# One scan and one step on r put ahead of the low part of a weight tile on VectorE, in a gated linear attention with an ELU feed-forward

## The chip, the cores and the metric

The kernel runs on one core of one Trainium2 chip. The metric is the device time in microseconds (us) of one execution; times of several executions are given as their median. Four engines compute: TensorE (PE in the rows, its weight loads PEld), VectorE (DVE), ScalarE (ACT) and GpSimd (POOL). SyncE (SP) issues nearly all DMAs.

## The reference

```python
B, H, S, D = 4, 8, 768, 48              # q, k, v, alpha: float32 (B, H, S, D)
for t in range(S):
    state = alpha[:, :, t, :, None] * state + einsum('bhd,bhe->bhde', k[:, :, t], v[:, :, t])
    y[:, :, t] = einsum('bhd,bhde->bhe', q[:, :, t], state)
x = y.transpose(0, 2, 1, 3).reshape(B * S, H * D)       # 3072 x 384
h = x @ w_in                                            # w_in 384 x 2048
g = where(h > 0, h, exp(minimum(h, 0)) - 1)
out = g @ w_out                                         # w_out 2048 x 384
```

The weights arrive as float64.

## The kernel before

**Tiling.** The attention is cut into 24 windows of 128 tokens, six for each batch entry. A window's step is named by two letters and its number i: L.i loads k, q and alpha; SC.i (L299, VectorE) makes P, the running products of alpha, by one scan; LN.i and EX.i (L311, L317, ScalarE) make R = 1/P; KA.i, KB.i and KC.i (L325, L330, L335) scale k; PC.i (L340, ScalarE) goes over P once more and keeps the sum of each partition for a check at the end; SQ.i scales q by P; U, S, MK, Y are the small matrix products and the mask, and UA, UB, UC (L509, L538, VectorE) carry the state on. The tokens then go through the feed-forward in nine blocks b, three of 256 tokens and six of 384, and each block over sixteen parts j of the 2048 inner columns (eight pairs in the narrow blocks): A.b.j (L786, TensorE) writes h into a PSUM bank, RA (L795) and RB (L800) on ScalarE make r = exp(min(h, 0)), RC (L806, VectorE) makes max(r - 1, h), GH (L812, ScalarE) and GL (L819, VectorE or GpSimd) split it into a high and a low part, and O.b.j (L835, TensorE) multiplies by w_out.

**Weights.** Sixteen tiles f: F.f loads the raw 64-bit words (L675), KW, DA and DB (L686, L702, L707) turn them into float32 in a tile called wm or spare, WH.f (L734, ScalarE) writes the high part and WL.f (L754, VectorE or GpSimd) the low part. F.13 and F.15 go into the memory of the tile spare and so wait until WL.9 and WL.11 have read it.

**What sets the order.** The order of the steps is a table written out by hand, the string ORDER. Its words are issued one after the other, each to its engine, and no scheduler changes the order on an engine. Two more strings say which of eight PSUM banks and which of eleven SBUF slots each tile takes. Around the change:

- A.1.4 takes the PSUM bank that held h of A.0.6, so TensorE may start A.1.4 when RC.0.6 has read it.
- P has two buffers. The scans stand in the order SC.3, SC.5, SC.4, SC.6, so SC.6 writes into the buffer of window 5. The last to read P of window 5 are SQ.5 on GpSimd and PC.5 on ScalarE.
- WLV (L43) puts WL.11 on VectorE and WL.9, WL.12, WL.14 on GpSimd.

```python
work = main.enter_context(tc.tile_pool(name="work", bufs=2))
...
        d["P"] = work.tile([128, NP, AW], F32, name="P", tag="P")            # SC
...
    nc.scalar.activation(out=win[i]["R"], in_=pw(i), func=AF.Copy, accum_out=chk_p[:, 1, i:i + 1])   # PC
...
    d["g"] = d["r"] if inr(b, j) else d["h"]                                 # RC
    nc.vector.scalar_tensor_tensor(out=d["g"], in0=d["r"], scalar=-1.0, in1=d["h"], op0=ALU.add, op1=ALU.max)
```

Of the kernel before, what the change touches and what calls it, by code (L numbers as in the profile page):

```python
# [15 lines left out]
B, H, S, D = 4, 8, 768, 48  # L16
# [51 lines left out]
CA.1 RC.1.2 KA.4 WH.5 WL.8 O.1.1 GH.1.2 WL.5 RA.1.3 RB.1.3 GL.1.2 A.1.5 RC.1.3 GH.0.3 F.14 ZV.6 KW.6 DA.6 CB.1 F.11  # L68
A.0.4 O.1.2 RA.0.4 RB.0.4 A.0.5 RA.1.5 O.0.2 KB.4 DB.6 WH.14 GL.0.3 SQ.4 KC.4 S.4 WH.12 RB.1.5 RA.0.5 RC.0.4 L.6 KC.5
RC.1.5 DA.5 GH.0.4 KW.5 LV.6 MK.4 TP.4 RB.0.5 GH.1.5 RC.0.5 KN.4 TP.5 KN.5 LC.3 DB.5 GH.1.3 O.0.3 PC.4 SQ.5 CA.3 LV.5  # L70
U.5 WH.9 WL.12 S.5 MK.5.1 MK.5.0 A.0.6 WH.11 WL.11 RA.0.6 GL.1.3 O.1.3 LV.4 U.4 RB.0.6 RC.0.6 PC.5 CB.3 SC.6 WL.9 LN.6
EX.6 GL.0.4 A.1.4 RA.1.4 RB.1.4 UA.4 UB.4 UC.4 L.7 SC.7 LN.7 KA.6 LC.2 RC.1.4 WL.14 A.1.6 KB.6 A.1.7 UA.5 GH.0.5 O.0.4
EX.7 KA.7 KB.7 RA.1.7 KC.6 RA.1.6 RB.1.7 RC.1.7 F.13 GH.1.4 GH.0.6 Y.5 RB.1.6 KC.7 T.7.2 GL.1.5 XH.5 Y.4 PC.7 RC.1.6
XH.4 XL.4 TP.6 GL.1.4 O.1.4 KN.6 F.15 DA.7 KW.7 O.1.5 U.6 UA.6 XL.5 DB.7 PC.6 SQ.6 S.6 MK.6.1 CA.2 GH.1.6 WH.13 GL.0.5
# [1021 lines left out]
```

## Time and profile before

| | |
|---|---|
| median of 3 runs | 463.38 us (463.38 to 463.59) |
| the profiled execution | 463.46 us, its span 461.7 us |
| TensorE busy | 453.9 us, 98% |
| VectorE busy | 349.6 us, 76% |
| ScalarE busy | 327.8 us, 71% |
| GpSimd busy | 214.5 us, 46% |
| granted TensorE clock, mean | 0.999 |

The span runs from the first to the last instruction of the profiled execution; 463.46 us is the time of that same execution with what lies around the span. Shares are over the whole span, so a full engine in one stretch and an empty one in another can give the same share. The times in the rows below count from the start of the span.

### The profile page before, as it was taken

The page shows a single profiled execution, that of the slowest core. Times are in us where ns is not written, and L with a number is a line of the kernel's source. Part 1 is how long each engine was busy: PE and PEld are TensorE (multiplying, and loading weights), DVE is VectorE, ACT ScalarE, POOL GpSimd, SP SyncE. Part 2 cuts the span into 40 slices and gives each one's busy share as a digit, 9 for nine tenths or more (in the row PEclk, how much of TensorE's full clock was granted, in tenths as well). Part 3 has the DMA queues.
Part 4 walks back from the last instruction along what each step waited for, and adds up shares of the span by engine and source line. Part 5 has one row for each costly group of instructions (what it writes and reads, how often), then busy time and mean ns, then how long its engine had stood idle before and what let it go on. Part 6 is the DMA issues. An engine that isn't in the chain of part 4 may idle for free.

```text
span 461.7 us, 12448 instructions
## 1 busy us (share of the span) xinstructions
PE 453.9 (98%) x4942; PEld 439.6 (95%) x4942; DVE 349.6 (76%) x756; ACT 327.8 (71%) x741; POOL 214.5 (46%) x185
## 2 busy tenths in 40 slices
PE   8999999999999999999999999999999999999996
PEld 4889999999999999999999999999999999999995
DVE  8989999999998979978888987898688643211431
ACT  4789997966655767776684976786867568647742
POOL 2224597668647557660744542672434031211140
PEclk9999999999999999999999999999999999999999
DMA  8997744353370535314154425424241311112101
GB/s 280 415 411 287 287 104 156 158 154 103 100 239 0 183 107 173 133 43 140 44 177 142 124 67 181 148 78 155 78 121 35 121 45 53 30 39 85 36 4 57
DMA packets 23859, 61.10 MB, mean 132 GB/s; under 512 B 3184, under 2 KB 10864, under 8 KB 23792
## 3 DMA queue, kind: packets, MB, share of 16 engines
q1 hardware_dynamic: 23360, 59.63, 38.6%
q8 instruction: 41, 0.67, 0.6%
q10 hardware_dynamic: 432, 0.59, 0.3%
q14 instruction: 26, 0.21, 0.2%
HBM read 53.52 MB, written 4.72 MB: 126 GB/s over the span
## 4 chain that ended last, share of the span: by engine, by line
PE 84%; ACT 6%; DVE 5%; issue 1%; DVEq 0%; ACTq 0%
PE o L835 37%; PE h L786 37%; PE y L556 4%; PE q L427 2%; PE q L472 2%; ACT w L734 1%; PE y L551 1%; ACT raw L686 1%; ACT r L800 1%; DVE raw L702 1%; DVE wm L707 1%; ACT gh L812 1%; ACT r L795 1%; DVE r L806 0%; DVE w L754 0%
## 5 line engine op out<-in xcount | busy, mean ns | idle before, releaser
L786 PE MATMUL h<-xt,w 128*128 128x384 f32 (+1 forms) x1296 | 199.9, 310 | 0.3 <-DVE r L806 0.3
L786 PEld LDWEIGHTS h<-xt,w 128*128 128x128 f32 x1296 | 190.7, 190 | 1.5 <-DVE r L806 0.4
L835 PE MATMUL o<-w,gh 128*128 128x384 f32 x768 | 188.3, 327 | 0.0
L819 POOL TENSOR_TENSOR gl<-r,gh 128x384 fp32r<-128x384 f32 (+1 forms) x90 | 106.7, 1193 | 157.7 <-ACT gh L812 101.3
L835 PEld LDWEIGHTS o<-w,gh 128*128 128x128 f32 x768 | 134.1, 189 | 0.5
L835 PE MATMUL o<-w,gl 128*128 128x384 f32 x384 | 125.2, 326 | 0.0
L795 ACT ACTIVATE r<-h 128x384 f32<-128x384 f32 (+1 forms) x120 | 60.4, 510 | 54.9 <-PE h L786 49.0
L388 DVE STREAM_TRANSPOSE kn<-qka 32x128 f32<-32x128 f32 x256 | 77.4, 303 | 4.2
L806 DVE SCALAR_TENSOR_TENSOR r<-r,h 128x384 f32<-128x384 f32 (+1 forms) x90 | 51.1, 578 | 37.7 <-ACT r L800 31.3
L835 PEld LDWEIGHTS o<-w,gl 128*128 128x128 f32 x384 | 72.6, 189 | 0.1
L800 ACT ACTIVATE r<-r 128x384 f32<-128x384 f32 (+1 forms) x120 | 64.1, 543 | 2.0
L812 ACT CAST gh<-r 128x384 fp32r<-128x384 f32 (+1 forms) x90 | 46.4, 529 | 18.5 <-DVE r L806 16.0
L356 POOL TENSOR_TENSOR st<-qka,P 64x512 f32<-64x512 f32 x34 | 43.0, 1265 | 17.4 <-DVE P L299 16.1
L455 DVE TENSOR_TENSOR st<-q,mask 64x256 f32<-64x256 f32 x76 | 32.1, 422 | 9.2 <-PE q L427 6.0
L325 POOL TENSOR_TENSOR qka<-qka,R 128x512 f32<-128x512 f32 x16 | 21.1, 1316 | 29.9 <-ACT R L317 24.7
L806 DVE SCALAR_TENSOR_TENSOR h<-r,h 128x384 f32<-128x384 f32 (+1 forms) x30 | 17.4, 586 | 20.8 <-ACT r L800 20.3
L299 DVE TENSOR_TENSOR_SCAN P<-qka,first 128x516 f32<-128x516 f32 (+1 forms) x25 | 30.7, 1232 | 0.5 <-DMA qka<-in_qka_dram 0.2
L819 DVE TENSOR_TENSOR gl<-h,gh 128x384 fp32r<-128x384 f32 (+1 forms) x30 | 17.3, 581 | 17.8 <-ACT gh L812 7.3
L725 ACT ACTIVATE ck<-ck,lim 128x384 f32<-128x384 int32 x32 | 25.7, 802 | 0.6
L720 ACT ACTIVATE ck<-ck,lim 128x384 int32<-128x384 int8 x32 | 25.4, 794 | 0.0
L311 ACT ACTIVATE R<-P 128x512 f32<-128x512 f32 (+1 forms) x25 | 15.4, 616 | 11.7 <-DVE P L299 11.6
L812 ACT CAST gh<-h 128x384 fp32r<-128x384 f32 (+1 forms) x30 | 14.8, 498 | 8.8 <-DVE h L806 7.9
(95 smaller groups left out, 455.4 us busy)
## 6 DMA issues: line engine op xcount, KB each, us to landing
qka<-in_qka_dram SPq DMA_DIRECT2D x18, 770.0 KB, 6.5
ck<-in_wgt_dram SPq DMA_DIRECT2D x32, 384.0 KB, 3.2
raw<-in_wgt_dram SPq DMA_DIRECT2D x16, 767.6 KB, 9.5
vs<-in_vv_dram SPq DMA_DIRECT2D x42, 192.0 KB, 3.8
out_dram<-ot SPq DMA_DIRECT2D x21, 192.0 KB, 1.9
qka<-in_qka_dram SPq DMA_DIRECT2D x4, 514.0 KB, 4.9
qka<-in_qka_dram SPq DMA_DIRECT2D x8, 256.0 KB, 3.8
xt<-y SPq DMA_DIRECT2D x40, 48.0 KB, 2.5
```

Of the source, the lines that this page charges most:

```text
L299: nc.vector.tensor_tensor_scan(out=P[:, n].rearrange("p n w -> p (n w)"), data0=t[:, 2 * NP * W + n.start * AW:2 * NP * W + n.stop * AW], ...
L356: eng(SQV, i).tensor_tensor(out=st[r, a], in0=d["q"][r], in1=pw(i)[r], op=ALU.mult)
L388: nc.vector.transpose(out=kn[32 * t:32 * t + 32, :, 32 * g:32 * g + 32], in_=d["kt"][32 * g:32 * g + 32, :, 32 * t:32 * t + 32])
L455: nc.vector.tensor_tensor(out=d["st"][r, a, :, c * C:(c + 1) * C], in0=d["s4"][a][o], in1=mask[o].unsqueeze(1).broadcast_to([64, NP, C]), ...
L725: nc.scalar.activation(out=t[:, :, 1].bitcast(F32), in_=t[:, :, 0], func=AF.Square, bias=lim[:, 1:2], accum_out=chk_w[:, f:f + 1])
L786: nc.tensor.matmul(h[:, y, :], lhsT=t[:, wi, ws], rhs=x[:, c, xi].rearrange("p (a x) -> p x a", a=2), start=(y == 0 and k == 0), stop=(k = ...
L795: nc.scalar.activation(out=r, in_=d["h"], func=AF.Relu, scale=-1.0)
L800: nc.scalar.activation(out=d["r"], in_=d["r"], func=AF.Exp, scale=-1.0)
L806: nc.vector.scalar_tensor_tensor(out=d["g"], in0=d["r"], scalar=-1.0, in1=d["h"], op0=ALU.add, op1=ALU.max)
L812: nc.scalar.copy(out=gh, in_=d["g"])
L819: q.tensor_tensor(out=gl, in0=d["g"], in1=d["gh"].bitcast(F32), op=ALU.subtract)
L835: nc.tensor.matmul(o[:, 0:DM], lhsT=gt[:, y, ms], rhs=t[:, wi, f * DM:f * DM + DM].rearrange("p (a x) -> p x a", a=2), start=(u == 0 and y ...
```

## The change

On VectorE, three neighbouring instructions change their order. Before: the low part of weight tile 11 (WL.11), the step on r of block 0, part 6 (RC.0.6), the scan of window 6 (SC.6). After: SC.6, RC.0.6, WL.11. In the table of words SC.6 moves ahead of RB.0.6 and so also ahead of PC.5, which stood before it; on every other engine the order of the instructions stays the same.

```diff
-U.5 WH.9 WL.12 S.5 MK.5.1 MK.5.0 A.0.6 WH.11 WL.11 RA.0.6 GL.1.3 O.1.3 LV.4 U.4 RB.0.6 RC.0.6 PC.5 CB.3 SC.6 WL.9 LN.6
+U.5 WH.9 WL.12 S.5 MK.5.1 MK.5.0 A.0.6 WH.11 RA.0.6 GL.1.3 O.1.3 LV.4 U.4 SC.6 RB.0.6 RC.0.6 WL.11 PC.5 CB.3 WL.9 LN.6
```

VectorE before, from the last mask of window 5 to the step UC.4; names carry their buffer numbers, the brackets name the engines and DMA queues whose semaphores an instruction waits for, and the scan (L299) is listed under its instruction's form:

```order
L455 TENSOR_TENSOR st_1083<-q_1102,mask_87 64x4x64
L754 TENSOR_TENSOR w5_1098<-spare7_476,w5_1098 128x768 [waits DVE_49,Activation_49]
L806 SCALAR_TENSOR_TENSOR r_1144<-r_1144,h_1123 128x512 [waits PE_49,Activation_49]
L299 SCALAR_TENSOR_TENSOR P_1183<-qka0_125,first_91 128x516 [waits DMAHW2_49,Activation_49,Pool_49]
L509 TENSOR_TENSOR vs0_109<-vs0_109,q_1161 128x192 [waits PE_49]
L509 TENSOR_TENSOR q_1162<-vs0_109,q_1162 128x192 [waits DVE_49,PE_49]
L538 TENSOR_TENSOR vs1_110<-q_1162,P_710 48x192 [waits DVE_49]
```

The same place in the change:

```order
L455 TENSOR_TENSOR st_1083<-q_1102,mask_87 64x4x64
L299 SCALAR_TENSOR_TENSOR P_1178<-qka0_125,first_91 128x516 [waits DMAHW2_49,Activation_49,Pool_49]
L806 SCALAR_TENSOR_TENSOR r_1143<-r_1143,h_1123 128x512 [waits PE_49]
L754 TENSOR_TENSOR w5_1098<-spare7_476,w5_1098 128x768 [waits DVE_49]
L509 TENSOR_TENSOR vs0_109<-vs0_109,q_1160 128x192 [waits PE_49]
L509 TENSOR_TENSOR q_1161<-vs0_109,q_1161 128x192 [waits DVE_49,PE_49]
L538 TENSOR_TENSOR vs1_110<-q_1161,P_710 48x192 [waits DVE_49]
```

The scan keeps its three waits and now stands first; the step on r and the low part stand behind it and no longer name ScalarE (Activation) themselves.

ScalarE in the change, from the high parts of tiles 9 and 11 to LN.6 of window 6 (P_605 is P of window 5, P_1178 that of window 6); the order is the same as before:

```order
L734 CAST w5_1098<-spare7_476 128x768
L795 ACTIVATE r_1143<-h_1123 128x512 [waits PE_49]
L800 ACTIVATE r_1143<-r_1143 128x512 [waits Activation_49]
L340 ACTIVATE R_712,chk_p_118<-P_605 128x512 [waits Pool_49]
L725 ACTIVATE ck_1065,chk_w_117<-ck_1065,lim_122 128x384
L311 ACTIVATE R_1186<-P_1178 128x512 [waits DVE_49]
```

PC.5 (L340, reading P_605) stands behind RB.0.6 (L800) and ahead of LN.6 (L311); nothing moved here.

## Rows read from the trace of the kernel before

**Rows 1.** Busy time by engine in four stretches: us, then busy us of each engine, granted clock
```profile
core 0: us, PE busy (x) PEld busy (x) DVE busy (x) ACT busy (x) POOL busy (x), PEclk, DMA share, GB/s
77.03:77.32 0.29, 0.00 (x2) 0.00 (x1) 0.29 (x2) 0.01 (x1) 0.29 (x1) 1.00 0.00 0
77.32:110.00 32.68, 32.68 (x368) 32.03 (x369) 31.48 (x60) 23.44 (x50) 24.16 (x17) 1.00 0.43 150
110.00:200.00 90.00, 90.00 (x1127) 88.08 (x1126) 80.59 (x197) 62.26 (x154) 57.23 (x50) 1.00 0.41 132
200.00:457.30 257.30, 257.30 (x2429) 253.67 (x2427) 167.15 (x403) 176.75 (x418) 95.64 (x87) 1.00 0.28 87
```

**Rows 2.** Chain that ended last, 74 to 84 us: start, us, what
```profile
74.13 0.40 DVE st L455
74.53 0.06 issue
74.59 1.84 DVE w L754
76.43 0.15 issue
76.58 0.70 DVE r L806
77.28 0.04 issue
77.32 6.29 PE h L786 x54
```

**Rows 3.** Timeline of TensorE, 76 to 89 us: start, us, operation, idle before and releaser
```profile
76.35 0.68 PE L472 MATMUL q<-vs,kn 64*64 64x48 f32 x32
77.32 6.29 PE L786 MATMUL h<-xt,w 128*128 128x256 f32 x54 [0.29 <-DVE r L806]
...
85.50 1.15 PE L556 MATMUL y<-st,vs 128*64 128x64 f32 x32
```

**Rows 4.** Timeline of ScalarE around the change
```profile
75.14 0.63 ACT L800 ACTIVATE r<-r 128x512 f32<-128x512 f32 x1
75.67 0.62 ACT L340 ACTIVATE R<-P 128x512 f32<-128x512 f32 x1
76.20 0.18 ACT L340 ACTIVATION_READ_ACCUMULATOR R<-P 128x1 f32 x1
...
78.80 0.64 ACT L311 ACTIVATE R<-P 128x512 f32<-128x512 f32 x1 [1.76 <-DVE P L299]
...
89.94 2.41 ACT L686 ACTIVATE raw<-raw 128x1536 int32<-128x1536 uint8 x1
```

**Rows 5.** Timeline of VectorE, 74 to 83 us
```profile
74.59 1.96 DVE L754 TENSOR_TENSOR w<-spare,w 128x768 fp32r<-128x768 f32 x1
76.58 0.69 DVE L806 SCALAR_TENSOR_TENSOR r<-r,h 128x512 f32<-128x512 f32 x1
77.18 1.59 DVE L299 TENSOR_TENSOR_SCAN P<-qka,first 128x516 f32<-128x516 f32 x1
78.69 0.32 DVE L509 TENSOR_TENSOR vs<-vs,q 128x192 f32<-128x192 f32 x1
...
80.28 1.23 DVE L299 TENSOR_TENSOR_SCAN P<-qka,first 128x516 f32<-128x516 f32 x1
81.42 0.67 DVE L325 TENSOR_TENSOR qka<-qka,R 128x512 f32<-128x512 f32 x1
82.12 0.69 DVE L806 SCALAR_TENSOR_TENSOR r<-r,h 128x512 f32<-128x512 f32 x1
82.73 0.73 DVE L509 TENSOR_TENSOR vs<-vs,q 48x192 f32<-48x192 f32 x2
```

**Rows 6.** Timeline of GpSimd: the three around the change, and one product alone
```profile
73.90 1.83 POOL L754 TENSOR_TENSOR w<-spare,w 128x768 fp32r<-128x768 f32 x1
75.69 1.99 POOL L819 TENSOR_TENSOR gl<-r,gh 128x512 fp32r<-128x512 f32 x1
77.64 2.76 POOL L754 TENSOR_TENSOR w<-wm,w 128x768 fp32r<-128x768 f32 x1
...
96.85 1.29 POOL L819 TENSOR_TENSOR gl<-r,gh 128x512 fp32r<-128x512 f32 x1 [0.34 <-POOL gl L819]
```

**Rows 7.** Timeline of VectorE at 54 us: a low part with GpSimd idle
```profile
54.31 0.95 DVE L754 TENSOR_TENSOR w<-spare,w 128x768 fp32r<-128x768 f32 x1
```

**Rows 8.** Timeline of SyncE: DMA issues behind the low part
```profile
77.50 0.84 SPq L675 DMA_DIRECT2D raw<-in_wgt_dram  x2
```

**Rows 9.** The tile raw, 60 to 120 us: its DMAs from issue to landing
```profile
DMA to landing us min/median/max: 4.4/5.2/5.9
```
## The prediction

> **What bounds the kernel now.** I first read the busy time by stretches. From 77.32 to 457.30 us TensorE is busy in every microsecond of each of the three stretches [rows 1]: 32.68 of 32.68, 90.00 of 90.00, 257.30 of 257.30, at a granted clock of 1.00. There is no slack after 77.32 us into which a late start could vanish. So whatever moves TensorE's start at 77.32 us should move the end by the same amount, in either direction.
>
> Next comes the chain that ended last. Just ahead of 77.32 it does not run over TensorE but over VectorE: the last mask, then the low part of weight tile 11 (WL.11, 1.84), then the step on r (RC.0.6, 0.70), then TensorE's A.1.4 [rows 2]. TensorE had finished its work before at 76.35 + 0.68 = 77.03 and stood idle for 0.29 us for that step [rows 3]. This is the place of the change: the step on r is what releases TensorE, and the change takes the 1.96 us of WL.11 [rows 5] from in front of it and puts a scan there instead.
>
> Then I read what the scan itself must wait for. Before, that could not be seen: SC.6 started at 77.18, at once behind the step on r. Its instruction names ScalarE and GpSimd beside its DMA. P has two buffers, SC.6 writes into the buffer of window 5, and the last reader on ScalarE is PC.5, which stands there behind RB.0.6. The instruction rows of the change agree: with the scan in front, the step on r no longer names ScalarE although it needs RB.0.6, so the scan's own wait must reach at least as far as RB.0.6. PC.5 starts at 75.67 and its accumulator is read out until 76.20 + 0.18 = 76.38 [rows 4]. ScalarE there depends on TensorE and on itself, not on the three moved instructions, so this time stays.
>
> **The change part by part.** It adds and removes no instruction; each of the three moved steps is one VectorE instruction and issues no DMA. The times below are those of the profiled execution (463.46 us, 0.08 above the median of 463.38).
>
> 1. *The scan waits.* VectorE is free for it at 74.59, where WL.11 stood [rows 5]. It can start only behind PC.5: 76.38 + 0.03 = 76.41, the 0.03 being the step from the end of the old scan (77.18 + 1.59 = 78.77) to LN.6 at 78.80 [rows 4, 5]. VectorE stands empty for 1.82 us, with the step on r and WL.11 queued behind the waiting scan.
>
> 2. *The scan's length.* It has two ends: 1.23 as at 80.28, start to start 81.42 - 80.28 = 1.14, and 1.59 as at 77.18, start to start 1.51 [rows 5]. The difference lies on GpSimd. At 77.18 GpSimd's product GL.0.4 ran until 75.69 + 1.99 = 77.68 [rows 6], and the scan ended at 78.77, that is 1.09 later: the 1.23 of a scan alone less 0.14 that it had already spent. WL.11 shows the same: GpSimd's WL.9 ended at 75.73, and WL.11, 0.95 alone [rows 7], ended at 76.55, 0.82 later. And GL.0.4, 1.29 alone [rows 6], ended 1.13 behind WL.11. So of two operations that read two operands from SBUF, the second one waits for the first, less some 0.15 us of its own start. After the change GL.0.4 starts at the same 75.69 (it waits for TensorE), has VectorE idle beside it, and ends at 75.69 + 1.29 = 76.98. The scan then ends at 76.98 + 1.09 = 78.07.
>    The Trainium skill has this rule in SBUF — State Buffer, "SBUF: two separate sides": VectorE's second read interface is GpSimd's too, and whoever starts first keeps it for the whole instruction while the other "fully blocks". The trace differs by the 0.14 above, in three pairs; taken to the letter it is a rival below.
>
> 3. *The step on r and TensorE.* The next instruction starts 0.08 before the end of the scan (78.69 against 78.77), so at 77.99; it takes 0.69 (77.27 in the old place) and TensorE starts 0.05 later [rows 3, 5]: 77.99 + 0.69 + 0.05 = 78.73, against 77.32. **TensorE starts 1.41 us later.** Its 0.29 us of idle time becomes 1.70. RB.0.6, which the step also needs, ended at 75.77 [rows 4] and no longer matters.
>
> 4. *The low part, now last.* It starts 0.09 before the end of the step, at 78.59. GpSimd's WL.14 (1.83, as WL.9 [rows 6]) is ready at 76.94 (0.04 before the end of the product ahead of it, as at 77.64), is held by the scan until 78.07 and ends near 79.7 (the old one ended at 80.40, 1.63 behind the old scan). WL.11 then ends at 79.70 + 0.82 = 80.52, and the state step UA.4 runs from 80.44 to 80.76, against 78.69 to 79.01 [rows 5]. TensorE's A.1.6 takes the bank that UA.4 reads. A.1.4 lasts a third of the 6.29 us for 54 products [rows 3], 2.10, so A.1.6 is due at 78.73 + 2.10 = 80.83 and UA.4 lets it go at 80.76 + 0.05 = 80.81. No wait comes on top, by 0.02 us; I keep 0 to 0.2 for the range.
>
> 5. *What else hangs on these.* VectorE stays 1.75 us late from there, TensorE 1.41, so TensorE's later waits lose 0.34 of their slack. The next is Y.5 at 85.50, which needs the state step that ended at 82.73 + 0.73 = 83.46 [rows 3, 5]: 2.0 us of slack. The DMAs F.13 and F.15 wait for WL.11, and the next load of k, q and alpha is queued behind them on SyncE; they were issued at 77.50 [rows 8] and now near 80.55 to 81.4. They land 4.4 to 5.9 us after issue [rows 9], by 87.3, and ScalarE opens them at 89.94 [rows 4] or later. Cost nothing. LN.6 starts near 78.1 instead of 78.80 [rows 4]; the RA.1.4 behind it waits for TensorE anyway.
>
> Sum: 463.46 + 1.41 = 464.87, and against the median **464.8 us** (463.38 + 1.41 = 464.79). The bounds of the scan's length: start to start 1.14 gives 76.41 + 1.14 + 0.69 + 0.05 = 78.29, +0.97, 464.35; the other end is the first rival. I take the value in step 2 since GpSimd's GL.0.4 is running when the scan becomes ready.
>
> **The rivals.**
>
> *The block is complete.* With no start saved, the scan ends at 76.98 + 1.23 = 78.21, TensorE starts at 78.87 (+1.55); WL.14 ends at 80.04, WL.11 at 80.99, UA.4 at 81.23, and A.1.6, due at 80.97, starts at 81.28: 0.31 more, +1.86 in all, 465.2. Against it: three pairs that each ended 0.13 to 0.16 earlier than that.
>
> *GpSimd goes first.* At 76.98 the scan has been waiting since 76.41, and GpSimd's WL.14 comes. If WL.14 took the turn, it would end at 76.94 + 1.83 = 78.77, the scan at 79.86, and TensorE would start at 79.78 + 0.69 + 0.05 = 80.52, +3.20, 466.6. Against it: at 77.68 the waiting scan went ahead of WL.14, which then took 2.76 [rows 6].
>
> *The scan does not wait* (the change does what the new order suggests). If its ScalarE wait were for something earlier than PC.5, the scan would start at 74.59 and, unhindered, be followed at 75.80 by the step on r (RB.0.6 ends at 75.77), which would end at 76.49, before TensorE needs it at 77.03. The 0.29 us of idle time would go: 463.1, not slower. The point that decides is whether the wait lies before 75.77 or behind it. For it: the rows name only the engine, not the instruction. Against it: the step on r has dropped its ScalarE wait, and the buffer's last reader is PC.5.
>
> *Part of it comes back.* TensorE could run later parts with fewer gaps. Its weight loads are not quite as full as its products, 32.03 of 32.68 in the first stretch [rows 1]. Those gaps recur where it changes from one kind of product to another and none is a wait that an earlier VectorE would end. A return of half, 464.1, is the most I would grant.
>
> **How the numbers follow.** Forecast (scan held by PC.5, +0.97 to +1.6): 0.76, its own range 464.3 to 465.0. Complete block, 465.2: 0.08. GpSimd first, 466.6: 0.04. No wait, 463.1: 0.08. Part back, near 464.1: 0.04. The range 464.1 to 465.5 holds the forecast, the complete block and part of the last case, and leaves out the no-wait case and GpSimd first. A measurement of this kernel can tell about 0.2% from no change, 0.93 us, so slower begins at 464.31. Slower: 0.76 + 0.08 + 0.04, less 0.03 for the lower edge of the forecast, 0.85. Within 0.2%: 0.08 + 0.04 and that 0.03, less 0.02, 0.13. Faster by more than that would take a gain of 0.93 us where TensorE idles 0.29: 0.02.
>
> **What would show it.** In the profile after: VectorE idle from about 74.55 to 76.4, ended by ScalarE's L340; the scan at 76.4 for about 1.65; the step on r at 78.0; TensorE's wait for it about 1.7 instead of 0.29, and A.1.4 at 78.7; WL.11 last, at 78.6, near 1.9 long; from there to the end the same full TensorE, 1.4 us later. A scan that starts at 74.6 would make the prediction wrong at step 1. A scan of 1.2 us would be wrong at step 2 only, and TensorE would start near 78.3. A second TensorE wait, at A.1.6, would show that step 4 was too close.

## The result and the profile after

Six executions of the changed kernel gave 466.53 us (median; 465.14 to 466.94), six of the kernel before beside them 463.48 (463.20 to 463.70): a ratio of 1.0059, 95% interval 1.0044 to 1.0074. The change makes the kernel slower, as forecast, but by more: 464.8 was predicted, with 464.1 to 465.5 as the range.

The six are not alike. Two of them, at 465.14 and 465.46 us, have a mean granted clock of 1.000; the other four lie at 466.51 to 466.94 with 0.994 to 0.996. The profiled execution (466.61 us, span 464.9) is one of the four. The work just ahead of the place of the change runs 0.12 us earlier in it than in the trace before.

VectorE after the change, timeline from 74 to 81 us (start, us, operation, idle before and releaser); it answers to [rows 5]:

```profile
74.01 0.43 DVE L455 TENSOR_TENSOR st<-q,mask 64x256 f32<-64x256 f32 x1
76.35 1.59 DVE L299 TENSOR_TENSOR_SCAN P<-qka,first 128x516 f32<-128x516 f32 x1 [1.91 <-POOL w L754]
77.97 0.69 DVE L806 SCALAR_TENSOR_TENSOR r<-r,h 128x512 f32<-128x512 f32 x1
78.57 1.79 DVE L754 TENSOR_TENSOR w<-spare,w 128x768 fp32r<-128x768 f32 x1
80.29 0.34 DVE L509 TENSOR_TENSOR vs<-vs,q 128x192 f32<-128x192 f32 x1
```

ScalarE and GpSimd at the same place, answering to [rows 4, 6]:

```profile
75.55 0.62 ACT L340 ACTIVATE R<-P 128x512 f32<-128x512 f32 x1
76.08 0.18 ACT L340 ACTIVATION_READ_ACCUMULATOR R<-P 128x1 f32 x1
```

```profile
73.78 1.83 POOL L754 TENSOR_TENSOR w<-spare,w 128x768 fp32r<-128x768 f32 x1
75.57 1.27 POOL L819 TENSOR_TENSOR gl<-r,gh 128x512 fp32r<-128x512 f32 x1
76.80 2.75 POOL L754 TENSOR_TENSOR w<-wm,w 128x768 fp32r<-128x768 f32 x1
```

The scan comes first and stands still for 1.91 us. The row puts this down to GpSimd's WL.9, which ended at 73.78 + 1.83 = 75.61, 0.74 us too early to be what ended last. PC.5's accumulator was read out at 76.08 + 0.18 = 76.26, and the scan starts 0.09 later. Here the name in the bracket is that of another wait of the same instruction; the ends of the candidates must be compared.

TensorE, timeline from 76 to 90 us, answering to [rows 3]:

```profile
76.23 0.68 PE L472 MATMUL q<-vs,kn 64*64 64x48 f32 x32
78.71 7.92 PE L786 MATMUL h<-xt,w 128*128 128x256 f32 x54 [1.80 <-DVE r L806]
...
88.51 1.15 PE L556 MATMUL y<-st,vs 128*64 128x64 f32 x32
```

Two things changed. TensorE now idles 1.80 us ahead of A.1.4 instead of 0.29. And the 54 products behind it take 7.92 us instead of 6.29, without a wait among them. The second is explained by the busy time by stretches, answering to [rows 1]:

```profile
core 0: us, PE busy (x) PEld busy (x) DVE busy (x) ACT busy (x) POOL busy (x), PEclk, DMA share, GB/s
76.91:78.71 1.80, 0.00 (x1) 0.01 (x1) 1.77 (x3) 0.71 (x2) 1.80 (x1) 1.00 0.35 77
78.71:79.70 0.99, 0.99 (x8) 0.99 (x9) 0.99 (x1) 0.64 (x2) 0.84 (x1) 0.95 0.64 258
79.70:83.00 3.30, 3.30 (x18) 3.30 (x17) 3.11 (x6) 0.81 (x2) 0.00 (x0) 0.50 0.43 115
83.00:85.00 2.00, 2.00 (x19) 2.00 (x19) 1.94 (x5) 2.00 (x5) 1.19 (x1) 1.00 1.04 427
85.00:110.00 25.00, 25.00 (x310) 24.35 (x309) 23.03 (x42) 17.69 (x38) 16.90 (x11) 1.00 0.36 119
```

TensorE is full from 78.71 on, but from about 79.6 to 83.0 us its granted clock is 0.50, the 1.2 GHz level: 18 products in 3.30 us, where the stretch at 1.00 behind it has 19 in 2.00. Before that it had stood empty for 1.80 us and worked for less than 1 us again. Half of these 3.4 us is 1.7 us of lost work; the lengths of the group give 7.92 - 6.29 = 1.63.

So the account of the profiled pair closes in the main: A.1.4 starts 1.80 - 0.29 = 1.51 us later behind the work before it, the half clock costs 1.63, together 3.14; measured 466.61 - 463.46 = 3.15. It closes better than the rows allow: since the work ahead of the place was 0.12 us early, Y.5 at 88.51 is only 3.01 us behind its old 85.50 [rows 3], and the last 0.14 us come between there and the end, where the trace shows no wait of TensorE.

### The profile page after: what moved, and what is told of

It is laid out like the page before. It is cut to its first block, busy times and chain, and to the rows that moved or that the text cites. A ratio compares the mean times of both kernels' runs of the same rounds, so it can differ in the third digit from the quotient of the medians.

```text
span 464.9 us, 12446 instructions
## 1 busy us (share of the span) xinstructions
PE 455.7 (98%) x4942; PEld 441.1 (95%) x4942; DVE 350.0 (75%) x756; ACT 327.5 (70%) x741; POOL 213.4 (46%) x185
## 4 chain that ended last, share of the span: by engine, by line
PE 88%; ACT 3%; DVE 3%; DMA 3%; issue 1%; POOL 1%; SPq 0%; POOLq 0%; DVEq 0%
PE h L786 39%; PE o L835 38%; PE y L556 4%; PE q L472 2%; PE q L427 2%; DMA vs<-in_vv_dram 2%; PE y L551 1%; ACT w L734 1%; DVE wm L707 1%; DMA qka<-in_qka_dram 1%; DVE P L299 1%; POOL gl L819 1%; PE y L605 1%; ACT gh L812 1%; PE sc L443 0%
## 5 line engine op out<-in xcount | busy, mean ns | idle before, releaser
L388 DVE STREAM_TRANSPOSE kn<-qka 32x128 f32<-32x128 f32 x256 | 77.5, 303 | 4.2
L800 ACT ACTIVATE r<-r 128x384 f32<-128x384 f32 (+1 forms) x120 | 64.0, 543 | 2.0
L299 DVE TENSOR_TENSOR_SCAN P<-qka,first 128x516 f32<-128x516 f32 (+1 forms) x25 | 30.9, 1235 | 2.7 <-POOL w L754 1.9
L311 ACT ACTIVATE R<-P 128x512 f32<-128x512 f32 (+1 forms) x25 | 15.3, 614 | 10.4 <-DVE P L299 10.3
```

The costliest lines, as they stand in the source:

```text
L299: nc.vector.tensor_tensor_scan(out=P[:, n].rearrange("p n w -> p (n w)"), data0=t[:, 2 * NP * W + n.start * AW:2 * NP * W + n.stop * AW], ...
L388: nc.vector.transpose(out=kn[32 * t:32 * t + 32, :, 32 * g:32 * g + 32], in_=d["kt"][32 * g:32 * g + 32, :, 32 * t:32 * t + 32])
L800: nc.scalar.activation(out=d["r"], in_=d["r"], func=AF.Exp, scale=-1.0)
```

## The experiments

The theory after this: VectorE stands still because the scan waits for PC.5, TensorE waits for the step on r, and idle time of TensorE costs its own length and, in part of the executions, a fall of the clock to 1.2 GHz behind it. The rivals: the low part WL.11, now last, makes the loss by itself; or the weight DMAs, which now run beside A.1.4 to A.1.7, slow the products down. An execution counts below as one that lost the clock if its mean granted clock is 0.996 or less; 3.4 us at half clock lower that mean by some 0.004. The kernel before shows that in 2 of 64 executions beside these runs. The profiled executions reach the place at different times (TensorE's last small products begin between 75.8 and 77.5 us), so waits are compared, not starts. Kernels with added code have other line numbers: L793 or L794 is A's line 786, L813 or L814 RC's 806, L761 WL's 754, L683 F's 675.

**1. PC.5 ahead of the scan.**

```diff
-U.5 WH.9 WL.12 S.5
+U.5 PC.5 WH.9 WL.12 S.5
...
-SC.6 RB.0.6 RC.0.6 WL.11 PC.5 CB.3 WL.9
+SC.6 RB.0.6 RC.0.6 WL.11 CB.3 WL.9
```

> The change with one more edit: PC.5, the ScalarE reader of the P buffer that the scan SC.6 overwrites, is put ahead of the high parts WH.9 and WH.11. Theory (the scan waits for PC.5, and the idle TensorE then loses clock): the scan starts near 74.5 us instead of 76.35, is held by GpSimd's WL.9 until about 75.6 and ends near 76.7; the step on r ends near 77.3, TensorE starts A.1.4 within 0.2 us of the kernel before, the granted clock stays 1.00, and the time is 463.4 to 463.8 us. Rival D (the slower A.1.4 to A.1.7 come from the DMAs F.13, F.15 and L.8, which now run beside them): they are issued near 79 us and still run beside A.1.6 and A.1.7, so 464.2 to 465. Rival W (a low part that comes last costs the time): WL.11 is still last, 465 or more.

Measured: 463.82 us (463.04 to 465.17, 12 executions), ratio 1.0000 (0.9982 to 1.0018); no execution lost the clock. VectorE's timeline of this kernel, and TensorE's:

```profile
74.03 2.22 DVE L299 TENSOR_TENSOR_SCAN P<-qka,first 128x516 f32<-128x516 f32 x1
76.28 0.69 DVE L806 SCALAR_TENSOR_TENSOR r<-r,h 128x512 f32<-128x512 f32 x1
76.89 1.25 DVE L754 TENSOR_TENSOR w<-spare,w 128x768 fp32r<-128x768 f32 x1
```

```profile
77.03 6.29 PE L786 MATMUL h<-xt,w 128*128 128x256 f32 x54 [0.56 <-DVE r L806]
```

The order on VectorE is that of the change, and its loss is gone but for 0.27 us of TensorE's wait (0.56 against 0.29), which puts the time 0.02 above what was expected. The scan starts at once behind the mask; it was PC.5 that it waited for. The low part is still last, so that position alone does not make the loss. The scan is 2.22 long because GpSimd's WL.9 runs beside it: that ended at 75.16 in this trace, and the scan 1.09 later, as in step 2 of the prediction.

**2. Idle time alone: five short writes in the kernel before.** They stand between WL.11 and RC.0.6 and touch a tile of their own.

```diff
+    dum = const.tile([128, 256], F32, name="dum")
+    @tok
+    def VD(n):
+        for _ in range(n):
+            nc.vector.memset(dum, 0.0)
...
-WL.11 RA.0.6 GL.1.3 O.1.3 LV.4 U.4 RB.0.6 RC.0.6 PC.5 CB.3 SC.6
+WL.11 RA.0.6 GL.1.3 O.1.3 LV.4 U.4 RB.0.6 VD.5 RC.0.6 PC.5 CB.3 SC.6
```

> The kernel before with five memsets of 128x256 on VectorE between WL.11 and RC.0.6, some 1.3 to 1.5 us; order, waits, DMAs and scan as before. Theory: TensorE idles 0.3 + 1.4 us, loses clock in most executions, and the time is 463.5 + 1.4 + 1.6, about 466.5, in those and about 465 in the others. Rival D: F.13 and F.15 are issued at 77.5 as before, the products are not slowed beyond that: 464.9 in all executions with clock 1.00.

Measured: 465.22 us (464.15 to 467.11, 7 executions), ratio 1.0038 (1.0021 to 1.0054). TensorE of the profiled execution, at clock 1.00 throughout:

```profile
79.53 6.29 PE L793 MATMUL h<-xt,w 128*128 128x256 f32 x54 [2.13 <-DVE r L813]
```

A miss in part. The idle time cost about its own length, 2.13 - 0.29 = 1.84 us in the trace and 1.6 between the medians, but only one execution of seven (467.11, at 0.996) lost the clock, although TensorE idled longer than in the change. The fall does not come in every execution, so one profile can miss it.

**3. TensorE kept busy in the gap.** In the changed kernel, twelve small bf16 products into unused columns of a bank stand ahead of A.1.4.

```diff
-EX.6 GL.0.4 A.1.4
+EX.6 GL.0.4 XW.4.12 A.1.4
...
+    def XW(i, n):
+        t = win[i]["q4"][0][0][:, 256:512]
+        for _ in range(n):
+            nc.tensor.matmul(t.rearrange("p (a x) -> p a x", a=2), lhsT=wz,
+                             rhs=wz.unsqueeze(1).broadcast_to([128, 2, 128]), start=True, stop=True,
+                             skip_group_check=True)
```

> The change with twelve idle products of 128x256 (bfloat16) put on TensorE ahead of A.1.4, into columns of a PSUM bank that nobody reads; they need no operand that comes late and fill about 77.0 to 78.6 us. Everything else waits as in the change. Theory: A.1.4 starts at 78.7 as in the change, but the clock stays at 1.00: 463.5 + 1.5, 464.9 to 465.2 us in all executions. Rival D: the DMAs still run beside A.1.4 to A.1.7, so 466.5 as the change.

Measured: 465.44 us (464.51 to 465.88, 6 executions), ratio 1.0034 (1.0021 to 1.0047); none lost the clock. TensorE:

```profile
77.64 1.48 PE L580 MATMUL q<-wz 128*128 128x256 bf16 x12
79.61 6.29 PE L794 MATMUL h<-xt,w 128*128 128x256 f32 x54 [0.49 <-DVE r L814]
```

```profile
81.33 0.80 SPq L683 DMA_DIRECT2D raw<-in_wgt_dram  x2
```

A.1.4 waits for the same step on r, and its 54 products are back at 6.29 us, though the weight DMAs are issued at the same place as in the change and run beside them. The DMAs do not slow the products; and what is left, some 1.8 us, is the late step on r. That the filling is what kept the clock, these six executions alone do not show: the unaltered change kept it in six of eleven (run 6).

**4. Useful work in the gap: O.0.4 ahead of A.1.4.**

```diff
-EX.6 GL.0.4 A.1.4
+EX.6 GL.0.4 O.0.4 A.1.4
...
-UA.5 GH.0.5 O.0.4
+UA.5 GH.0.5
```

> The change with the product O.0.4 moved ahead of A.1.4 on TensorE: real work of about 2 us, whose operands are there by 76.9 us, fills the wait for the step on r. Theory: TensorE is busy from 77.0 on, A.1.4 starts near 79.0 without a wait, the clock stays at 1.00, and the time is 463.1 to 463.6 us. Rival D: the DMAs run beside A.1.4 to A.1.7 as in the change, so 464.8 to 465.2. If A.1.6 or A.1.7 wait for the late state steps, up to 0.5 more.

Measured: 465.86 us (464.88 to 466.75, 6 executions), ratio 1.0048 (1.0033 to 1.0063); two of six lost the clock, the profiled one among them. The gain that was expected did not come. TensorE's timeline, and the busy time of the stretch behind its wait:

```profile
78.99 6.19 PE L786 MATMUL h<-xt,w 128*128 128x256 f32 x54
...
90.06 0.78 PE L378 MATMUL tp<-ident,qka 128*128 128x128 f32 x4 [1.75 <-DVE r L806]
```

```profile
88.00:90.06 2.06, 0.32 (x11) 0.18 (x7) 2.03 (x3) 1.11 (x5) 2.06 (x2) 1.00 0.00 0
90.06:93.70 3.64, 3.63 (x14) 3.64 (x15) 3.53 (x9) 2.79 (x8) 1.78 (x2) 0.56 0.00 0
```

A.1.4 no longer waits, but at 90 us TensorE waits 1.75 us for a later step on r. VectorE and GpSimd show why; the last two lines are VectorE's same two products in the kernel before:

```profile
85.22 1.66 DVE L325 TENSOR_TENSOR qka<-qka,R 128x512 f32<-128x512 f32 x1
87.52 1.77 DVE L335 SCALAR_TENSOR_TENSOR qka<-R,qka 128x512 f32<-128x512 f32 x1
89.32 0.69 DVE L806 SCALAR_TENSOR_TENSOR r<-r,h 128x512 f32<-128x512 f32 x1
```

```profile
85.05 1.28 POOL L819 TENSOR_TENSOR gl<-r,gh 128x512 fp32r<-128x512 f32 x1
87.47 1.27 POOL L819 TENSOR_TENSOR gl<-r,gh 128x512 fp32r<-128x512 f32 x1 [1.14 <-ACT gh L812]
```

```profile
83.49 0.69 DVE L325 TENSOR_TENSOR qka<-qka,R 128x512 f32<-128x512 f32 x1
84.82 0.69 DVE L335 SCALAR_TENSOR_TENSOR qka<-R,qka 128x512 f32<-128x512 f32 x1
```

In the kernel before, GpSimd's product waited for TensorE's O (2.36 us, until 85.71) and so came behind both of VectorE's. With O.0.4 done early it no longer waits, and two of GpSimd's products each start just ahead of one of VectorE's. VectorE's end 0.55 us behind them and take 0.97 and 1.08 us longer than before. The step on r at 89.32 is the one at 85.54 before [rows 5], 3.78 us later: 1.73 is how late VectorE already was (83.85 against 82.12), 2.05 are these two holds. Without them it would have ended near 87.96 (an estimate from these rows; no run takes them away), ahead of the 88.32 at which TensorE ran out of work in this trace. So the late step on r was filled, and the work moved forward opened a new gap by what it set off on GpSimd. The clock fell there too, and with a DMA share of 0.00, so it is not the DMAs that lower it either.

**5. A shorter idle time: two writes instead of five** (`VD.2` in the edit of run 2).

> The kernel before with two short VectorE writes (0.37 us each in the run with five) between the low part and the step on r, so TensorE should stand idle for 0.29 + 0.74 = 1.0 us ahead of A.1.4. Theory (an idle time of TensorE costs its own length, and from some length on in part of the executions also a stretch at half clock): +0.7, 464.2 us, granted clock 1.00 in all or nearly all executions. Rival (any idle time here loses the clock): 465.5 us and more, with the clock below 0.997 in half of the executions.

Measured: 465.19 us (465.00 to 465.58, 5 executions), ratio 1.0039 (1.0025 to 1.0053); none lost the clock. Half of the expectation missed: 1 us of idle time was to cost 0.7. TensorE, VectorE's scan and GpSimd's WL.14:

```profile
78.28 2.27 PE L793 MATMUL h<-xt,w 128*128 128x256 f32 x18 [1.01 <-DVE r L813]
81.14 4.29 PE L793 MATMUL h<-xt,w 128*128 128x256 f32 x36 [0.59 <-DVE vs L509]
```

```profile
78.14 2.71 DVE L299 TENSOR_TENSOR_SCAN P<-qka,first 128x516 f32<-128x516 f32 x1
```

```profile
77.93 1.83 POOL L761 TENSOR_TENSOR w<-wm,w 128x768 fp32r<-128x768 f32 x1
```

The two writes delayed the scan just enough for WL.14 to start 0.21 us ahead of it. The scan then ended at 80.85, 1.09 us behind WL.14's 79.76, the state step came late, and A.1.6 waited a second time, 0.59. The two waits, 1.01 + 0.59 - 0.29 = 1.31, are most of the 1.69 between the medians; the rest has no row that I found. This is close to the rival "GpSimd goes first", though here WL.14 had started before the scan was ready and did not overtake it, and it is the second wait of step 4, both in a kernel built for another question. The Trainium skill, SBUF — State Buffer, "SBUF: two separate sides", says that whoever starts first keeps the shared pair for the whole instruction; by that rule the order of two starts 0.21 us apart decides over 1.8 us, and this trace agrees, less the 0.14 of step 2.

**6. The change once more,** unaltered.

> The change once more, unaltered, to count how often its executions show the lower clock. Theory (the idle time of 1.8 us alone gives 465.1 to 465.5, and the half clock comes on top in part of the executions, as by chance): some executions at clock 1.00 near 465.3, others near 466.6 with 0.994 to 0.996; the share is open, 4 of 6 so far. Rival (this order of the work loses the clock always, and the two executions near 465.3 were exceptions): at least 5 of 6 near 466.6.

Measured: 465.25 us (464.80 to 466.36, 5 executions), ratio 1.0043 (1.0030 to 1.0057). One of five lost the clock. The profiled execution did not, TensorE and the stretch at 80 us:

```profile
79.00 6.29 PE L786 MATMUL h<-xt,w 128*128 128x256 f32 x54 [1.91 <-DVE r L806]
```

```profile
80.00:83.00 3.00, 3.00 (x29) 3.00 (x28) 2.81 (x6) 1.23 (x2) 0.00 (x0) 1.00 0.37 92
```

The same kernel, an idle time 0.11 us longer, and no fall: 29 products in 3.00 us. Over both comparisons the change lost the clock in 5 of 11 executions. The six that kept it lie at 464.80 to 465.46, middle 465.2; the five that lost it at 466.36 to 466.94, middle 466.55.

**7. The step on r ahead of the scan.**

```diff
-SC.6 RB.0.6 RC.0.6 WL.11 PC.5 CB.3 WL.9
+RB.0.6 RC.0.6 PC.5 CB.3 SC.6 WL.11 WL.9
```

> The change with the step on r ahead of the scan (order on VectorE: step on r, scan, low part). The scan still waits for PC.5, but the step on r is no longer queued behind it, so TensorE starts A.1.4 without a wait, near 77.05. The low part stays ahead of the state step UA.4 and holds it until about 80.7, while A.1.6 is due at 77.05 + 2.10 = 79.15: theory, TensorE waits there about 1.5 us inside the 54 products, and the time is near 464.7 with the clock kept, 466 and more where it is lost. Rival (the cost of the change lay in the late start of A.1.4 alone): 463.1 to 463.5.

Measured: 464.77 us (464.45 to 464.96, 7 executions), ratio 1.0029 (1.0018 to 1.0040); none lost the clock. VectorE, then TensorE:

```profile
75.50 0.69 DVE L806 SCALAR_TENSOR_TENSOR r<-r,h 128x512 f32<-128x512 f32 x1 [1.19 <-ACT r L800]
76.17 1.65 DVE L299 TENSOR_TENSOR_SCAN P<-qka,first 128x516 f32<-128x516 f32 x1
77.75 2.51 DVE L754 TENSOR_TENSOR w<-spare,w 128x768 fp32r<-128x768 f32 x1
```

```profile
76.66 2.27 PE L786 MATMUL h<-xt,w 128*128 128x256 f32 x18
80.58 4.29 PE L786 MATMUL h<-xt,w 128*128 128x256 f32 x36 [1.65 <-DVE vs L509]
```

As expected: A.1.4 starts without a wait, and A.1.6 waits 1.65 us for the state step behind the low part, whose 2.51 us are again WL.14's turn. 1.65 - 0.29 = 1.36, measured 1.27.

**8. The low part behind the steps on the state.**

```diff
-SC.6 RB.0.6 RC.0.6 WL.11 PC.5 CB.3 WL.9
+RB.0.6 RC.0.6 PC.5 CB.3 SC.6 WL.9
...
-UA.4 UB.4 UC.4 L.7
+UA.4 UB.4 UC.4 WL.11 L.7
```

> As the run with the step on r first, but with the low part moved behind the three steps on the state (order on VectorE: step on r, scan, UA, UB, UC, low part). Then neither A.1.4 nor A.1.6 should wait: the step on r runs near 75.8, TensorE starts at 77.05 without its 0.29 us of idle time, the state step ends near 78.4. Theory (both of the waits came from what stood ahead of the step on r and of the state step): 463.0 to 463.5, clock 1.00 as in the kernel before. Rival (VectorE's 1.2 us of standing empty comes back later as a wait, as in the run that filled TensorE's idle time): 464.2 or more.

> The order step on r, scan, three steps on the state, low part once more, unaltered, since its first comparison left 0.9987 to 1.0005 open. The most that it can give is TensorE's idle time ahead of A.1.4 in the kernel before, 0.29 us or 0.06%: expected 463.0 to 463.4, not told from the kernel before. A result at 462.5 or below would show a further gain that these theories do not have.

Measured: 463.24 us (462.82 to 464.13, 11 executions), ratio 0.9996 (0.9987 to 1.0005), and in the second comparison 462.91 (462.61 to 464.38, 11 executions), 0.9992 (0.9983 to 1.0002). VectorE and TensorE of the first:

```profile
76.25 1.61 DVE L299 TENSOR_TENSOR_SCAN P<-qka,first 128x516 f32<-128x516 f32 x1
77.78 0.33 DVE L509 TENSOR_TENSOR vs<-vs,q 128x192 f32<-128x192 f32 x1
...
79.36 0.96 DVE L754 TENSOR_TENSOR w<-spare,w 128x768 fp32r<-128x768 f32 x1
```

```profile
76.74 6.29 PE L786 MATMUL h<-xt,w 128*128 128x256 f32 x54
```

Neither A.1.4 nor A.1.6 waits, and the low part runs at its length alone, 0.96 [rows 7]. About 2 us better than the change; from the kernel before it cannot be told, and the 0.29 us of idle time that it removes [rows 3] is all that these theories give. The second median lies 0.09 below what was expected, still above the 462.5 that would have shown a further gain.

**9 and 10. A longer idle time,** by eight writes in the kernel before (`VD.8` in the edit of run 2), and by four in the change:

```diff
-U.4 SC.6 RB.0.6 RC.0.6 WL.11
+U.4 SC.6 VD.4 RB.0.6 RC.0.6 WL.11
```

> The kernel before with eight short VectorE writes (0.37 us each) between the low part and the step on r: TensorE should stand idle for 0.29 + 2.95 = 3.2 us ahead of A.1.4, and not a second time. The idle time alone gives 463.5 + 2.95 = 466.4. Theory (the chance that the clock falls to half behind an idle time grows with its length): at least half of the executions near 468 with the clock at 0.994 to 0.996. Rival (the change loses its clock for another reason than the length of the idle time, since the kernel with five such writes idled 2.13 us and lost it in 1 of 7): no more than 1 or 2 of the executions lose it, median near 466.4.

> The change with four short VectorE writes between the scan and the step on r: idle time of TensorE 1.8 + 1.5 = 3.3 us, about as in the run with eight writes but in the order of the change. The idle time alone gives 465.2 + 1.5 = 466.7. Theory (length of the idle time): at least half of the executions near 468.3 with the clock at 0.994 to 0.996, as in the run with eight writes. Rival (something in the order of the change): here clearly more of the executions lose the clock than in the run with eight writes.

Measured: 468.50 us (467.62 to 470.28, 4 executions), ratio 1.0102 (1.0087 to 1.0117), and 467.94 (467.50 to 470.09, 6 executions), ratio 1.0105 (1.0089 to 1.0121). All ten executions lost the clock. TensorE's timeline and the stretch at half clock, first of the kernel with eight writes, then of the change with four:

```profile
81.41 8.92 PE L793 MATMUL h<-xt,w 128*128 128x256 f32 x54 [3.25 <-DVE r L813]
```

```profile
80.40:86.50 6.10, 5.09 (x24) 5.09 (x25) 5.21 (x9) 2.16 (x5) 0.72 (x2) 0.50 0.98 401
```

```profile
80.25 7.73 PE L793 MATMUL h<-xt,w 128*128 128x256 f32 x54 [3.25 <-DVE r L813]
```

```profile
79.90:83.10 3.20, 2.85 (x13) 2.85 (x14) 3.01 (x7) 0.00 (x0) 0.00 (x0) 0.50 0.27 44
```

Both idle for 3.25 us, and at this length the order of the three instructions makes no difference to how often the clock falls. The clock fell here before TensorE had resumed its work. The two stretches shown lie inside the half clock: read in steps of 0.05 us it lasts from 80.1 to 86.95 us in run 9 and from 79.85 to 83.3 in run 10.

**11. Run 2 once more,** since its 1 of 7 did not fit between 5 of 11 and 10 of 10.

> The kernel before with five short VectorE writes once more, unaltered, since 1 of 7 executions at 2.13 us of idle time does not fit between 5 of 11 at 1.8 to 1.9 us (the change) and 10 of 10 at 3.25 us. If the chance of the lower clock goes by the length of the idle time alone, about half of the executions or more should show 466.5 to 467.2 at a clock of 0.994 to 0.996, and the 1 of 7 was chance. If it is again 0 or 1 of 6 or 7, near 465.2, something beside the length counts, and it stays open what.

Measured: 465.55 us (464.46 to 468.22, 7 executions), ratio 1.0059 (1.0037 to 1.0080); two of seven lost the clock (467.56 and 468.22). Neither of the two expectations is met. By length of idle time, read in one profiled execution of each kernel, these runs together give:

| idle time of TensorE at one place | kernels | lost the clock |
|---|---|---|
| up to 1.0 us | runs 1, 3, 5 | 0 of 23 |
| 1.65 us | run 7 | 0 of 7 |
| 1.75 to 1.91 us | the change (5 of 11), run 4 (2 of 6) | 7 of 17 |
| 2.13 us | run 2, twice | 3 of 14 |
| 3.25 us | runs 9, 10 | 10 of 10 |

The ends are clear. The rows of 1.75 to 1.91 and of 2.13 us stand in the wrong order, but 3 of 14 and 7 of 17 are too few to tell apart, and so are 0 of 7 at 1.65 and 7 of 17; the table gives no limit, and whether something beside the length counts there stays open.

## Why the prediction was right in direction and wrong in size

- **Step 1, the scan waits for PC.5: right.** PC.5 ended at 76.26 and the scan started at 76.35; predicted, in the time of this trace (0.12 earlier), were 76.26 and 76.29. Run 1 shows the cause by taking it away. The rival in which the scan does not wait falls with it. Its 463.1 was also too low by the prediction's own step 2: a scan that starts at 74.59 would have been held by WL.9 until 75.73, as run 1's scan was, and run 1 measured 463.82.
- **Step 2, the scan's length: right.** GL.0.4 follows WL.9 at once in both traces [rows 6], so it is WL.9 that sets its start, not a wait for TensorE; the number stays. GpSimd's GL.0.4 ended at 75.57 + 1.27 = 76.84 and the scan at 77.94, 1.10 later (1.09 predicted). The rival of the complete block falls here. "GpSimd goes first" did not happen in this kernel; run 5 shows what a scan behind WL.14 takes, 2.71 us instead of 1.59.
- **Step 3, TensorE's start: short by 0.10.** The wait is 1.80 us where 1.70 was predicted. The step on r did not start 0.08 ahead of the scan's end, as the state step does [rows 5], but 0.03 behind it (77.97 against 77.94).
- **Step 4, the low part last: right.** WL.11 ended at 80.36, 0.81 behind WL.14's 79.55 (0.82 predicted); the state step started at 80.29; A.1.6 did not wait. In this trace the half clock made A.1.6 late; in run 6, at full clock, the state step ended at 80.92 and A.1.6 was due at 79.00 + 2.10 = 81.10, and it did not wait there either.
- **Step 5, what else hangs on these: right.** Y.5 follows at 88.51 with no wait of its own. SyncE issued the weight DMAs at 80.43, and the last had landed long before ScalarE, without a wait, opened the tile at 92.95.
- **The sentence that failed stands in "What bounds the kernel now": "whatever moves TensorE's start at 77.32 us should move the end by the same amount".** It took the granted clock of 1.00 in [rows 1] as given. That clock was read in a kernel where TensorE idles 0.29 us there. With 1.80 us of idle time it fell to 1.2 GHz for 3.4 us in the profiled execution, which cost 1.63 us more; in all, 5 of 11 executions show the fall in their mean clock, and their middle lies 1.35 us above that of the other six. In none of the rivals did the clock appear, so the range ended 1 us short of the median. TensorE's being full is no proof that a late start is passed on one to one; a full engine can also be a slow one.

Where the clock was kept, the change stands at 465.2 against 463.5, +1.7 where +1.41 was predicted. Of these 0.3 us step 3 explains 0.10. The trace of run 6, which kept the clock, has a wait of 1.91 us, 0.11 more than in the first trace: GpSimd's GL.0.4 ended there at 75.86 + 1.27 = 77.13, 0.03 us behind TensorE's last small product instead of 0.07 ahead of it, and the scan 1.10 behind GL.0.4 as in step 2. The last 0.1 us is not settled. The median of 466.5 and the 465.25 of the second comparison differ by how many executions of each happened to lose the clock, four of six and one of five. The rival "part of it comes back" is wrong in sign.

The Trainium skill, TensorE: Matmul & The Clock Gate, "Part 1: The HAM clock gate (the "warmup" mystery)", says that the low clock is the default state and activity releases it, and that the same kernel can come out differently from run to run, since the hardware's view of the activity does not begin with the kernel. The traces agree in so far as half clock follows idle time and full clock comes back under work, and as one kernel with nearly the same wait shows either outcome (1.80 us with the fall, 1.91 us without); why it does, no run here shows.

## What to carry to other kernels

Before an instruction is moved ahead, find the last reader of the buffer it writes, on every engine: on an engine that works in order, a wait at the front holds everything behind it, and here the scan kept from TensorE a step on r that had been ready. Where TensorE is the bound, price a new gap twice, once for its length and once for the chance that the clock falls behind it, and compare several executions with their clocks: one profile shows one of two outcomes. And if a gap is filled with work from further behind, ask what that work releases on the other engines when it comes early: in run 4 it opened a second gap nearly as long as the first.

## What was not expected of the hardware

The clock can stay at 1.00 for almost 1 us after TensorE has resumed, and fall only then, in the middle of full work (0.95 from 78.71 to 79.70 us, 0.50 from 79.6 to 83.0), so the slow stretch does not stand beside the gap that it follows. And its length is not fixed: 3.4 us at half clock in the traces of the change, of run 4 and of run 10, and 6.8 in run 9, which has the same 3.25 us of idle time as run 10.
